# First expert of a routed network: its list of tokens taken behind round two of four, gathered before the search ends; eleven low parts made by GpSimd

## The chip, the cores and the metric

The kernel runs on one core of one Trainium2 chip. The metric is the device time of one execution in microseconds (us). A core has five engines that work beside each other, each through its own instructions in order: TensorE (PE, with its weight loads as PEld), VectorE (DVE), ScalarE (ACT), GpSimd (POOL) and SyncE (SP), which here issues loads. DMA queues move data between them and the chip's memory.

## What is computed

An attention over pooled keys and values gives 4608 tokens of 512 numbers. A gate scores each token against 8 experts. In the order of falling scores, a pair (token, expert) is taken if the token is free and the expert has fewer than 576 tokens. Each expert is a network of two layers, run on its own tokens alone.

```python
logits = x @ w_gate
order = np.argsort(-logits.flatten())
for idx in order:
    tok, e = (int(idx) // E, int(idx) % E)
    if assigned[tok] >= 0 or counts[e] >= cap:      # cap = 4608 // 8 = 576
        continue
    assigned[tok] = e
    counts[e] += 1
for e in range(E):
    mask = assigned == e
    out[mask] = np.maximum(x[mask] @ w1[e], 0.0) @ w2[e]
```

## The kernel before, in words

**Stages.** Attention runs over 36 tiles of 128 tokens and stores each tile of x in memory (`xd`). Then the experts run one after the other, each in two stages of products on TensorE, while the search for the next expert's tokens runs in between on VectorE and TensorE. No sort is made: the search finds which expert fills up first and at which score.

**The search** (`Routing.search`). The best score of each token is scaled to a number `q`. A round compares all q with 32 thresholds (`cmp`, VectorE), counts the tokens over each threshold for each expert (36 small products into `rt`, TensorE), asks which counts exceed what the expert still takes (`g`), and by one product and a maximum gets `up`, the step of the threshold. The next round divides that step by 32 again. There are four rounds. Behind the fourth, `sel` marks the tokens over the threshold and `full` the expert that is full.

**The close** (`Routing.close`). `fm` names the expert, `own` marks its tokens, `inc` and `si` number them by a running sum, `eid` is the expert's number as an address. The list itself is made by products with zero-one matrices: `OHb` holds which block of 32 entries a token falls in, and its number, `OHa` the place in the block. Nine products give the list, eight small ones (with `spread`) turn it into `rows`, the row numbers of five tiles of at most 128 tokens. For the first expert this is done in two parts, of two and three tiles. The rest of the close sums up what each expert still takes (`left`), checks (`bad`), and takes the chosen tokens and the full expert out of the scores (`lg`).

**An expert** (`Experts`). SyncE loads the weights w1 behind `eid` (`load_1`, the first expert's in two halves) and w2 (`load_2`). Each f32 number is split in a high part (`w1h`, `w2h`, ScalarE) and a low part (`w1l`, `w2l`, VectorE: raw minus high), in eight pieces of 512 columns; a product of two such numbers is three products. GpSimd gathers the token rows (`xg`, one indirect DMA for each tile), TensorE transposes them (`tp`), ScalarE and VectorE make `xh` and `xl`. Stage one multiplies by w1: for f = 0 to 7, a block of twelve products (w1h by xh, w1l by xh, w1h by xl, four each) into a tile `h`, for the columns 0 to 256 (tiles 0 and 1) and for the columns 256 to 576. ScalarE writes `hh` from it and VectorE `hl`. Tiles `h` rotate through five buffers, so that a block starts when the fifth one before it has been read. Stage two multiplies by w2 and scatters the rows out.

**What sets the order.** Every engine's order is written out by the program. The function `experts` walks through the products of a stage, adds up what they take by its own estimate (`now`, `dve`, `ready`), and between two products issues what is due: steps of the search (each `yield` of `Routing` hands over such a step with estimates), pieces of the weights (`Pieces`), transposes (`turn`), and the low parts of h (`later`). Before the first expert's products it works off the list and the first two tiles, with warming products (`warm`) in between. For the first expert the blocks ran in halves: f 0 to 3 of the columns 0 to 256, f 0 to 3 of the rest, then f 4 to 7 of both.

If the check in `bad` is not zero at the end, all experts are run again one by one with an exact search.

Of the kernel before, what the change touches and what calls it, by code (L numbers as in the profile page):

```python
# [423 lines left out]
class Routing:  # L424
# [7 lines left out]
    def __init__(self, tc, cst, wk, psR, lg, cap):  # L432
        self.tc, self.nc, self.cst, self.wk, self.psR = tc, tc.nc, cst, wk, psR
        self.lg = lg
        self.poke = None
        self.NC = lg.shape[1]
        self.cap = cap
# [175 lines left out]
    def search(self, shadow, spare):  # L613
# [18 lines left out]
        for k in range(rounds):  # L632
# [15 lines left out]
            else:  # L648
                compare(0, 2, 5, nb)
            if 0 < k < rounds - 1:  # L650
# [32 lines left out]

# [12 lines left out]
            nc.vector.tensor_reduce(up, ps[:, :8], axis=AX.X, op=OP.max)  # L696
            if k + 1 < rounds:
# [5 lines left out]
        nc.vector.tensor_scalar(self.sel, q16, up, 1.0 + EDGE, op0=OP.subtract, op1=OP.is_gt)  # L703

# [10 lines left out]
    def close(self, k, last):  # L715
# [7 lines left out]
        if k:  # L723
            nc.vector.tensor_tensor(self.code, self.code, new, op=OP.add)
        own = wk.tile([128, NC], F32, name="own")
        nc.vector.tensor_scalar(own, self.code if k else new, fm, None, op0=OP.is_equal)

        inc = wk.tile([128, NC], BF, name="inc")
        nc.vector.tensor_tensor_scan(inc, self.ones[:, :NC], own, 31.0, op0=OP.mult, op1=OP.add)
        eid = wk.tile([1, 1], I32, name="eid", bufs=3)  # L730
        nc.vector.tensor_scalar(eid, fm[:1], -1.0, 8.0, op0=OP.mult, op1=OP.add)
        nc.vector.tensor_scalar(eid, eid, 7.0, None, op0=OP.min)
        self.eid = eid
        yield 2.2, 2.2, "id"
        if not k:
            nc.vector.tensor_tensor(self.code, self.code, new, op=OP.add)
        ps = self.psum()
        nc.tensor.matmul(ps[:, :1], self.untri, self.ones[:, :1], start=True, stop=False)
        nc.tensor.matmul(ps[:, :1], self.tri, inc[:, NC - 1:NC], start=False, stop=True)

        si = wk.tile([128, NC], I32, name="si")
        nc.vector.scalar_tensor_tensor(si, inc, ps[:, :1], own, op0=OP.add, op1=OP.mult)
        sab = wk.tile([128, 2, NC], I32, name="sab")
        nc.vector.tensor_scalar(sab[:, 1], si, 5, None, op0=OP.arith_shift_right)
        nc.vector.tensor_scalar(sab[:, 0], si, 31, None, op0=OP.bitwise_and)
        sf = wk.tile([128, 2, NC], F16, name="sf")
        nc.vector.tensor_copy(sf.rearrange("p v (b q) -> p v b q", q=4), sab.rearrange("p v (q b) -> p v b q", q=4))
        if self.poke:

# [753 lines left out]
```

## Time and profile before

| what | value |
|---|---|
| runs before the change | 611.56 to 613.07 us, median 612.68 |
| profiled execution | 612.35 us, of which the span of the profile is 609.9 us |
| share of the span that is busy: PE, DVE, ACT, POOL | 97%, 65%, 39%, 29% |
| mean granted TensorE clock | 0.984 |
| stage-one products (L1093), three groups of 512 | 93.2, 93.4, 91.0 us |
| stage-two products (L1127), three groups of 256 | 101.8, 101.4, 101.5 us |
| low part of w1 (L1049, VectorE) | 64 of 685 ns |
| low part of w2 (L1058, VectorE) | 64 of 682 ns |
| low part of h (L1101, VectorE) | 128, mean 451 ns |
| gathers (L1037, GpSimd) | 40, mean 982 ns to issue |

The profile is of one execution. A row of its timeline gives the start and the length of an instruction in us from the span's start, the engine, the line of the kernel, the operation, out<-in by the program's names with their sizes, and in brackets how long the engine had been idle and what it had waited for. A row of stretches gives the busy time of each engine in a stretch of time. Groups of one line (page and groups) give count, busy time, mean length in ns and the idle time before them. TensorE is busy nearly always, so only the time in which it isn't can be saved: most of that lies between the end of attention (some 135 us) and the first expert's products.

### The profile page before, as it was taken

Reading aid. Unit: us, or ns where it says so; the run is one execution under the profiler, and the core shown is the slowest. Engines: PE = TensorE matmul, PEld = TensorE weight load, DVE = VectorE, ACT = ScalarE, POOL = GpSimd, SP = SyncE. Lnnn points to the kernel's source line nnn. Section 1 sums busy time; section 2 is a strip of 40 time slices with the busy share of each in tenths; the row PEclk is TensorE's granted clock in tenths of the full one; section 3 lists DMA queues with packets and bytes.
Section 4 is the critical chain, followed back from the end, with each engine's and each line's share of the span. In section 5 each row is a group of like instructions: output and inputs, shape, how many; then the busy total and the mean of one; then the engine's idle time right before and its main releaser. Section 6 shows DMA issues by size and latency. Waiting matters only on the chain.

```text
span 609.9 us, 11520 instructions
## 1 busy us (share of the span) xinstructions
PE 591.5 (97%) x4340; PEld 518.3 (85%) x4340; DVE 396.1 (65%) x1164; ACT 240.0 (39%) x562; POOL 177.3 (29%) x222
## 2 busy tenths in 40 slices
PE   8999999985999999999999999999999999999996
PEld 5999999983797799779977987898799889888975
DVE  7578888987885778767964976487367328503500
ACT  7444444461461434233432452255135325513411
POOL 2999999001200500420312301130221123011012
PEclk9999999995999999999999999999999999999999
DMA  8999972223531740616403701540081037014011
GB/s 353 419 420 423 397 274 82 77 100 98 167 116 31 254 147 22 213 62 219 134 35 116 284 1 52 207 174 18 36 323 57 34 120 278 2 52 166 1 40 43
DMA packets 32641, 92.23 MB, mean 151 GB/s; under 512 B 3488, under 2 KB 3488, under 8 KB 29888
## 3 DMA queue, kind: packets, MB, share of 16 engines
q1 hardware_dynamic: 21296, 62.92, 27.5%
q0 software_dynamic: 5952, 19.01, 9.2%
q10 hardware_dynamic: 5328, 9.48, 4.1%
q8 instruction: 35, 0.57, 0.4%
q14 instruction: 30, 0.25, 0.1%
HBM read 72.53 MB, written 18.87 MB: 150 GB/s over the span
## 4 chain that ended last, share of the span: by engine, by line
PE 81%; issue 7%; DVE 4%; DMA 3%; POOL 3%; ACT 1%; SPq 0%; POOLq 0%; ACTq 0%; another core or an unknown queue 0%; DVEq 0%
PE h L1093 32%; PE h L1127 25%; PE psa L272 6%; PE pss L227 5%; PE h L1132 4%; PE tp L1069 3%; DMA rawk<-in_k_dram 2%; PE pse L256 2%; PE rt L256 1%; PE rt L668 1%; DMA out_dram<-yt,rows 1%; PE rt L630 1%; DMA xg<-xd,rows 1%; PE rt L217 1%; DVE e L238 1%
## 5 line engine op out<-in xcount | busy, mean ns | idle before, releaser
L1127 PE MATMUL h<-w2l,hh 128*128 128x512 f32 x256 | 101.8, 398 | 0.0
L1127 PE MATMUL h<-w2h,hh 128*128 128x512 f32 x256 | 101.4, 396 | 0.3 <-PEq L1193 0.3
L1127 PE MATMUL h<-w2h,hl 128*128 128x512 f32 x256 | 101.5, 396 | 0.0
L1107 POOL DMA_INDIRECT out_dram<-yt,rows x29 | 30.3, 1045 | 232.3 <-ACT yt L1141 231.9
L1098 ACT ACTIVATE hh<-h 128x320 fp32r<-128x320 f32 (+1 forms) x128 | 52.5, 410 | 106.6 <-PE h L1093 103.3
L1093 PE MATMUL h<-xh,w1h 128*128 128x320 f32 (+1 forms) x512 | 93.2, 301 | 0.2 <-ACT xh L1071 0.2
L1093 PE MATMUL h<-xl,w1h 128*128 128x320 f32 (+1 forms) x512 | 93.4, 300 | 0.0
L1101 DVE SCALAR_TENSOR_TENSOR hl<-h,hh 128x320 fp32r<-128x320 f32 (+1 forms) x128 | 57.2, 451 | 53.1 <-ACT hh L1098 34.6
L1093 PE MATMUL h<-xh,w1l 128*128 128x320 f32 (+1 forms) x512 | 91.0, 298 | 0.0
L1093 PEld LDWEIGHTS h<-xh,w1h 128*128 128x128 f32 x512 | 75.7, 190 | 3.4 <-issue 2.7
L1093 PEld LDWEIGHTS h<-xl,w1h 128*128 128x128 f32 x512 | 76.1, 190 | 0.4
L1093 PEld LDWEIGHTS h<-xh,w1l 128*128 128x128 f32 x512 | 75.8, 189 | 0.0
L1037 POOL DMA_INDIRECT xg<-xd,rows x40 | 39.3, 982 | 101.9 <-DVE halves L806 52.7
L1141 ACT ACTIVATE yt<-h 128x512 f32<-128x512 f32 x32 | 19.1, 598 | 112.1 <-PE h L1127 67.4
L272 PE MATMUL psa<-vblk,eT 128*128 128x146 f32 (+3 forms) x390 | 59.9, 302 | 0.2
L1127 PEld LDWEIGHTS h<-w2h,hh 128*128 128x128 f32 x256 | 48.2, 188 | 9.3 <-issue 0.7
L1127 PEld LDWEIGHTS h<-w2l,hh 128*128 128x128 f32 x256 | 48.3, 189 | 8.8
L1127 PEld LDWEIGHTS h<-w2h,hl 128*128 128x128 f32 x256 | 48.2, 188 | 8.8
L272 PEld LDWEIGHTS psa<-vblk,eT 128*128 128x128 f32 (+1 forms) x390 | 50.9, 180 | 1.8 <-issue 0.3
L1049 DVE TENSOR_TENSOR w1l<-raw,w1h 128x512 fp32r<-128x512 f32 x64 | 41.7, 685 | 13.4 <-ACT w1h L1045 13.1
L1073 DVE TENSOR_TENSOR xl<-tp,xh 128x512 fp32r<-128x512 f32 (+1 forms) x40 | 25.3, 633 | 37.4 <-ACT xh L1071 37.3
L1058 DVE TENSOR_TENSOR w2l<-raw,w2h 128x512 fp32r<-128x512 f32 x64 | 43.2, 682 | 2.0 <-ACT w2h L1055 1.8
(224 smaller groups left out, 903.3 us busy)
## 6 DMA issues: line engine op xcount, KB each, us to landing
raw<-in_moe_w_dram SPq DMA_DIRECT2D x64, 512.0 KB, 6.3
xd<-xt ACTq DMA_DIRECT2D x36, 256.0 KB, 5.6
rawv<-in_v_dram SPq DMA_DIRECT2D x7, 1280.0 KB, 14.1
rawk<-in_k_dram SPq DMA_DIRECT2D x7, 1152.0 KB, 11.7
rawq<-in_q_dram SPq DMA_DIRECT2D x7, 1152.0 KB, 11.8
rawk<-in_k_dram SPq DMA_DIRECT2D x2, 576.0 KB, 4.7
rawv<-in_v_dram SPq DMA_DIRECT2D x1, 768.0 KB, 8.0
rawq<-in_q_dram SPq DMA_DIRECT2D x1, 640.0 KB, 9.0
```

The costliest lines, as they stand in the source:

```text
L227: nc.tensor.matmul(ps[cols, j // 2, 144 * (j % 2):144 * (j % 2) + 144], self.q_of(b, j, n, cols.stop - cols.start), self.kblk[b % 4][:, j] ...
L272: self.nc.tensor.matmul(o[h], self.eT[i][:, c, h], self.vblk[b % 4][:, self.BLOCKS[c]:self.BLOCKS[c + 1]], start=(c == cs[0]), stop=(c == ...
L1037: nc.gpsimd.indirect_dma_start(out=self.xg[:n, t, :], out_offset=None, in_=self.xd, in_offset=bass.IndirectOffsetOnAxis(ap=rows[:n, t:t + ...
L1049: self.nc.vector.tensor_tensor(l, raw, h.bitcast(F32), op=OP.subtract)
L1058: self.nc.vector.tensor_tensor(self.w2l[:, i], self.raw2[e][:, i], self.w2h[:, i].bitcast(F32), op=OP.subtract)
L1073: later(1.3, 0.65, lambda: nc.vector.tensor_tensor(xl, ps[:, :, :n], xh, op=OP.subtract))
L1093: nc.tensor.matmul(ps[:, :m], a[:, j, fs], b[:, j, o], start=(n == 0), stop=(n == 11))
L1098: nc.scalar.activation(hh[:, f, o], ps[:, :m], AF.Relu)
L1101: later(0.65, 0.4, lambda f=f, o=o, m=m, ps=ps: nc.vector.scalar_tensor_tensor(hl[:, f, o], ps[:, :m], 0.0, hh[:, f, o].bitcast(F32), op0= ...
L1107: st = nc.gpsimd.indirect_dma_start(out=rows, out_offset=bass.IndirectOffsetOnAxis(ap=idx, axis=0), in_=y, in_offset=None)
L1127: nc.tensor.matmul(ps, a[:, f, o], b[:, f], start=(f == 0 and k == 0), stop=(f == 7 and k == 2))
L1132: nc.tensor.matmul(ps[64 * a:64 * a + 64, :256], self.hr[:, f], self.raw2[e][:, f, 256 * a:256 * a + 256], start=(f == 0), stop=(f == 7))
```

## The change

The first expert's search is cut open behind its second round.

- **The early list** (`early`). What lies over the threshold of round two is taken as the first expert's already. From these tokens `eid`, `si` and two parts of the list are made, for the tiles 0 and 1 and the tiles 2 and 3 (512 tokens), and gathered. The rounds three and four come behind that in program order; the second part's small products stand within round three.
- **The late list** (`close` with `late`). Behind round four the tokens that are not among the first 512 (`taken`) get a short list of 64 for the fifth tile. Seven steps (`odd`) check that nothing else differs.
- **Stage one of the first expert** runs the blocks of the columns 0 to 256 four at a time, by kind: for f 0 to 3 all w1h by xh, then all w1l by xh, then all w1h by xl; then f 4 to 7; then the columns 256 to 576 for all f one by one.
- **GpSimd** makes three low parts of w1 and all eight of w2 for the first expert, eleven in all. VectorE made them before.
- Other experts keep their order but for one place where waiting low parts of x are issued by a fixed product (`lowered`).

```diff
@@ search @@
             else:
                 compare(0, 2, 5, nb)
+                if k == 2:
+                    rest = self.list_part(8, 16, self.bank)
+                    next(rest)
...
                 count(early, NC)
+                if k == 2:
+                    yield from rest
...
             nc.vector.tensor_reduce(up, ps[:, :8], axis=AX.X, op=OP.max)
+            if k == 1 and not spare:
+                yield from self.early(ps, up, q16)
...
+    def early(self, ps, up, q16):
+        nc, wk, NC = self.nc, self.wk, self.NC
+        full = wk.tile([128, 8], F32, name="full")
+        nc.vector.scalar_tensor_tensor(full, ps[:, :8], up, self.wts, op0=OP.is_ge, op1=OP.mult)
+        sel = wk.tile([128, NC], BF, name="sel")
+        nc.vector.tensor_scalar(sel, q16, up, 1.0 + EDGE, op0=OP.subtract, op1=OP.is_gt)
+        self.fm0 = fm = wk.tile([128, 1], F32, name="fm")
+        nc.vector.tensor_reduce(fm, full, axis=AX.X, op=OP.max)
+        own = wk.tile([128, NC], F32, name="own")
+        nc.vector.scalar_tensor_tensor(own, self.want, fm, sel, op0=OP.is_equal, op1=OP.mult)
+        inc = self.scan(own)
+        self.name(fm)
+        yield 2.2, 2.2, "id"
+        si = self.order(inc, own)
+        self.planes(si)
+        self.rows = wk.tile([128, 5], I32, name="rows", bufs=3)
+        self.block(0, 8)
+        self.number(0, 8)
+        self.lanes()
+        self.block(8, 16)
+        yield 2.6, 2.6
+        part = self.list_part(0, 8, self.bank)
+        next(part)
+        self.number(8, 16)
+        yield 0.6, 0.6
+        yield from part
+        self.taken = wk.tile([128, NC], F32, name="taken", bufs=1)
+        nc.vector.scalar_tensor_tensor(self.taken, si, 32.0 + 512.0, own, op0=OP.is_lt, op1=OP.mult)
...
@@ close, late @@
+        if late:
+            more = wk.tile([128, NC], F32, name="moreown", bufs=1)
+            nc.vector.scalar_tensor_tensor(more, self.taken, 0.0, own, op0=OP.is_equal, op1=OP.mult)
+            both, own = own, more
...
+        if late:
+            odd = wk.tile([128, 3], F32, name="odd", bufs=1)
+            nc.vector.tensor_tensor(both, both, self.taken, op=OP.subtract)
+            nc.vector.tensor_reduce(odd[:, 0:1], both, axis=AX.X, op=OP.min)
+            nc.vector.tensor_reduce(odd[:, 1:2], si, axis=AX.X, op=OP.max)
+            nc.vector.tensor_tensor(odd[:, 2:3], fm, self.fm0, op=OP.subtract)
+            nc.vector.scalar_tensor_tensor(self.bad, odd[:, 0:1], odd[:, 0:1], self.bad, op0=OP.mult, op1=OP.add)
+            nc.vector.scalar_tensor_tensor(self.bad, odd[:, 1:2], 32.0 + 64.0, self.bad, op0=OP.is_ge, op1=OP.add)
+            nc.vector.scalar_tensor_tensor(self.bad, odd[:, 2:3], odd[:, 2:3], self.bad, op0=OP.mult, op1=OP.add)
...
@@ Experts.low1, low2 @@
-        self.nc.vector.tensor_tensor(l, raw, h.bitcast(F32), op=OP.subtract)
+        (eng or self.nc.vector).tensor_tensor(l, raw, h.bitcast(F32), op=OP.subtract)
...
@@ stage1 @@
-        for o, some in ((cols[0], range(4)), (cols[1], range(4)), (cols[0], range(4, 8)), (cols[1], range(4, 8))) if (
-                halves) else ((cols[0], range(8)), (cols[1], range(8))):
+        for o, u in ((slice(0, 256), together), (slice(256, 576), 1)):
...
+            for f0 in range(0, 8, u):
+                ps = {}
+                for k, (a, b) in enumerate(((self.w1h, self.xh), (self.w1l, self.xh), (self.w1h, self.xl))):
+                    for f in range(f0, f0 + u):
...
@@ experts @@
-    for i in range(4):
-        w1.next(i < 3)
-    since[0, "rows"] = -7.0
-
+    turned[0] = 0
+    since[0, "rows"] = -7.0
+    for i in range(4):
+        w1.up()
     step(0)
-    warm(6)
+    step(0)
+    warm(4)
+    X.load_1(behind(0), 2, 4)
+    w1.next(False)
+    w1.next(False)
     now = dve = -1.0
-    for t in range(2):
-        turn(0, t)
-        warm(2)
-    flush()
+    turn(0, 0)
+    w1.next(False)
     step(0)
+    turn(0, 1)
+    flush(1)
+    w1.next(False)
+    warm(2)
...
-        w2 = Pieces(e, X.high2, X.low2)
-        for n, dt in enumerate(X.stage1(later, not e)):
+        w2 = Pieces(e, X.high2, X.low2, not e)
+        for n, dt in enumerate(X.stage1(later, 1 if e else 4)):
...
+            if not e and n == 22:
+                for i in range(4, 7):
+                    X.high1(0, i)
+                    X.low1(0, i, nc.gpsimd)
+                w1.h = w1.l = 7
+            if not e and n == 46:
+                w1.next()
```

The helpers `scan`, `name`, `order`, `planes`, `block`, `number`, `lanes` and `list_part` hold the same steps as the close did before, cut up for use in both places.

**TensorE before the first product.** The names: `g` and `ones` make the sums behind a round, `ones` into `h` is a warming product, `tp` are a tile's transposes, `cmp` a count. Before:

```order
L798 MATMUL rt<-cp,spread 128x3
...
L526 MATMUL h<-ones 128x512
...
L1069 MATMUL tp<-ident,xg 128x128 x4
...
L526 MATMUL h<-ones 128x512
...
L1069 MATMUL tp<-ident,xg 128x128 x4
...
L814 MATMUL rt<-pc,ones 128x8
L1093 MATMUL h<-xh,w1h 128x256 x4
L1093 MATMUL h<-xh,w1l 128x256 x4
```

And now, from the end of round three:

```order
L812 MATMUL h<-cp,spread 128x2
L699 LDWEIGHTS ones
L699 MATMUL rt<-g_247,ones 128x8
...
L527 MATMUL h<-ones 128x512
L1145 MATMUL tp<-ident,xg 128x128 x4
L631 LDWEIGHTS cmp
L631 MATMUL rt<-oh_259,cmp 32x8
...
L1145 MATMUL tp<-ident,xg 128x128 x4
...
L1170 MATMUL h<-xh,w1h 128x256 x2
L699 LDWEIGHTS ones
L699 MATMUL rt<-g_248,ones 128x16
L1170 MATMUL h<-xh,w1h 128x256 x14
```

The 36 counting products of round four stand between the transposes of the first and the second tile; the sum behind that round stands within the first block. The warming products are four and two, where they were six, two and two.

**VectorE in the close, around the low part of the block f = 4.** `left` to `lg` is the close, `odd` the new check, `hl` the low part of h. Before, at the end of the close:

```order
L825 TENSOR_REDUCE two<-sel 128x1
L826 SCALAR_TENSOR_TENSOR bad<-two,bad 128x1
L829 TENSOR_SCALAR pick<-full,fm 128x8
...
L838 TENSOR_TENSOR lg<-lg,pen_2143 128x288
L839 TENSOR_TENSOR lg<-lg,pen_2145 128x288
L1101 SCALAR_TENSOR_TENSOR hl<-h,hh 128x256
```

And now:

```order
L893 SCALAR_TENSOR_TENSOR bad<-two,bad 128x1
L896 TENSOR_TENSOR own<-own,taken 128x36
L897 TENSOR_REDUCE odd<-own 128x1
L898 TENSOR_REDUCE odd<-si 128x1
L899 TENSOR_TENSOR odd<-fm 128x1
L900 SCALAR_TENSOR_TENSOR bad<-odd,bad 128x1
...
L914 TENSOR_TENSOR lg<-lg,pen_2357 128x288
L915 TENSOR_TENSOR lg<-lg,pen_2359 128x288
L1182 SCALAR_TENSOR_TENSOR hl<-h,hh 128x256 x3
```

The low parts of the blocks f = 4 to 6 now stand behind the close with its seven more steps. On TensorE the block that takes the buffer of f = 4 is h_2405 (names with their numbers, from the close's sum on; h_2252 is f = 4, h_2382 and h_2405 are f = 0 and 1 of the columns 256 to 576):

```order
L880 MATMUL rt_2333<-pc_2308,ones_74 128x8
L1170 MATMUL h_2252<-xl_2062,w1h_2021 128x256
L1170 MATMUL h_2264<-xl_2062,w1h_2021 128x256 x4
L1170 MATMUL h_2269<-xl_2062,w1h_2021 128x256 x4
L1170 MATMUL h_2296<-xl_2062,w1h_2021 128x256 x4
L1170 MATMUL h_2382<-xh_2061,w1h_2021 128x320 x4
L1170 MATMUL h_2382<-xh_2061,w1l_2022 128x320 x4
L1170 MATMUL h_2382<-xl_2062,w1h_2021 128x320 x4
L1170 MATMUL h_2405<-xh_2061,w1h_2021 128x320 x4
```

Between the sum and h_2405 stand 13 products of 256 and 12 of 320 columns.

**GpSimd.** `norow` is a small gather whose data nobody uses. Before, the five gathers stood together and the first scatters followed; now:

```order
L1233 DMA norow<-in_moe_w_dram,sab 32x512
L1113 DMA xg<-xd,rows 128x512 x4
L1125 TENSOR_TENSOR w1l<-raw_1892,w1h 128x512 x3
L1113 DMA xg<-xd,rows 64x512
L1134 TENSOR_TENSOR w2l<-raw_2288,w2h 128x512 x8
L1187 MEMSET spacer 1x1
```

The fifth gather stands behind three low parts of w1, the eight of w2 behind that gather.

More of the change, by code (lines that the diff above doesn't have):

```diff
@@ L713, in chosen, with close @@
         return pc
-    def close(self, k, last):
+    def close(self, k, last, late=False):
         nc, wk, NC, lg = self.nc, self.wk, self.NC, self.lg
@@ L722, in close @@
         nc.vector.tensor_tensor(new, sel, self.want, op=OP.mult)
-        if k:
+        if not late:
             nc.vector.tensor_tensor(self.code, self.code, new, op=OP.add)
         own = wk.tile([128, NC], F32, name="own")
[L726 to L730, printed above, removed]
@@ L812, in close @@
+        self.number(0, n)
+        self.lanes()
+        yield (2.1, 2.1) if late else (2.6, 2.6)
+        part = self.list_part(0, n, self.psum, 5 - n // 4)
+        next(part)
+        if not late:
+            self.pc = self.chosen(sel)
+        yield (0.6, 0.6) if late else (1.75, 1.75)
+        yield from part
+        if late:
+            nc.vector.tensor_tensor(self.code, self.code, new, op=OP.add)
+            self.pc = self.chosen(sel)
             yield 1.15, 1.15
-            ps = self.psum()
@@ L885, in phase @@
             pass
-        yield from self.close(k, last)
+        yield from self.close(k, last, k == 0)
     def suspect(self):
@@ L1254, in step @@
                 toks[p] = R.rows, R.halves
-                turned[p] = 0
+                turned.setdefault(p, 0)
+                if not p:
+                    what = "late"
         since[p, what] = now
@@ L1322, in turn @@
         nonlocal now
-        now = max(now, since[e, "rows"] + 6.0 + 1.3 * t) + 0.45
+        now = max(now, comes(e, t)) + 0.45
         flush(1)
@@ L1328, in turn, with comes @@
         if (e, t) == (0, 2):
-            later(1.0, 0.2, lambda: X.load_1(behind(0), 2, 4))
-        elif (e, t) == (0, 4):
             later(1.0, 0.2, lambda: X.load_2(behind(1)))
+    def comes(e, t):
+        if (e, t) == (0, 4):
+            return since[0, "late"] + 3.7 if 0 in toks else 1e9
+        return since[e, "rows"] + 6.0 + 1.3 * t
     def turns(e, upto, late):
@@ L1336, in turns @@
         t = turned.get(e, 5)
-        if t < upto and due(e, "rows", 6.5 + 1.3 * t) and now >= last + 1.4 and (fresh or through or t < late):
+        if t < upto and (e or (0, "late") in since) and (e, "rows") in since and now >= comes(e, t) + 0.5 and now >= last + 1.4 and (fresh or through or t < late):
             last = now
@@ L1343, in warm @@
         R.warm(n, psB.tile([128, 512], F32, name="h", bufs=5))
[L1345 removed]
+    R.bank = lambda: psB.tile([128, 512], F32, name="h", bufs=5)
+    while R.found[1] < 4:
         step(0)
```

240 lines of the change are left out of this document (135 added, 105 removed).

## The prediction

> **What bounds the kernel.** I read the page's chain first, then busy time by stretches, then the timeline of the 30 us in which attention ends and the first expert begins.
>
> ```profile
> PE 81%; issue 7%; DVE 4%; DMA 3%; POOL 3%; ACT 1%; SPq 0%; POOLq 0%; ACTq 0%; another core or an unknown queue 0%; DVEq 0%
> ...
> 140.00:145.00 5.00, 2.64 (x62) 2.28 (x61) 3.39 (x19) 0.00 (x0) 0.00 (x0) 0.50 0.01 3
> ...
> 157.12:185.40 28.28, 28.28 (x226) 27.59 (x227) 24.37 (x75) 14.63 (x37) 0.00 (x0) 1.00 0.34 119
> 185.40:605.50 420.10, 419.59 (x2893) 361.66 (x2891) 247.16 (x746) 151.46 (x357) 78.19 (x113) 1.00 0.33 113
> ```
>
> TensorE carries 81% of the chain that ended last. The stretches give start:end, length, busy time of PE, PEld, DVE, ACT and POOL, granted clock, DMA. TensorE is busy through all 28.28 us of the first expert's stage one and 419.59 of the 420.10 us behind it. Only the hole before 157.12 can be won; and what stage two of the first expert starts earlier is won at the end, unless something behind it is late.
>
> The hole is a chain: four rounds (`up` ends each), the list (`rows`), the gather, the transposes, the first product.
>
> ```profile
> 138.60 0.14 DVE L696 TENSOR_REDUCE up<-rt 128x1 f32<-128x8 f32 x1
> ...
> 143.91 0.17 DVE L696 TENSOR_REDUCE up<-rt 128x1 f32<-128x8 f32 x1 [0.26 <-PE rt L694]
> 144.52 0.20 DVE L722 TENSOR_TENSOR new<-sel,want 128x36 f32<-128x36 bf16 x1
> 145.33 0.14 DVE L732 TENSOR_SCALAR eid<-eid 1x1 int32<-1x1 int32 x1
> 146.85 1.00 SPq L1020 DMA_DIRECT2D raw<-in_moe_w_dram  x2
> 149.33 0.16 DVE L802 TENSOR_SCALAR rows<-rt 128x2 int32<-128x2 f32 x1
> ...
> 150.34 0.97 POOL L1037 DMA_INDIRECT xg<-xd,rows  x1 [3.10 <-DVE rowd L782]
> 151.05 2.72 PE L526 MATMUL h<-ones 128*128 128x512 bf16 x6
> 151.18 2.38 ACT L1045 ACTIVATE w1h<-raw 128x512 fp32r<-128x512 f32 x4 [12.34 <-DMA raw<-in_moe_w_dram]
> 151.62 0.95 POOL L1037 DMA_INDIRECT xg<-xd,rows  x1 [0.30 <-issue]
> 153.83 0.68 PE L1069 MATMUL tp<-ident,xg 128*128 128x128 f32 x4
> 155.78 0.66 PE L1069 MATMUL tp<-ident,xg 128*128 128x128 f32 x4 [0.83 <-DMA xg<-xd,rows]
> 157.12 0.74 PE L1093 MATMUL h<-xh,w1h 128*128 128x256 f32 x4 [0.25 <-ACT xh L1071]
> ```
>
> Round two's `up` starts at 138.60, round four's at 143.91: the two rounds that the list no longer waits for are 5.31 us.
>
> **The start.** From `up` to `rows` it took 5.42. The early list needs the same steps without `new` (0.20): rows at 138.60 + 5.22 = 143.82. The gather began 1.01 behind rows and the next 1.28 behind it, now 144.83 and 146.11; their data were there 3.49 and 4.16 behind their starts, now 148.32 and 150.27. The weights came 1.52 + 4.33 behind `eid`, the expert's number, which moves up by as much: by 146.
>
> TensorE is not there that soon, for its order puts rounds three and four in between. One round, and the small products that turn list entries into rows:
>
> ```profile
> 136.41 0.90 DVE L625 TENSOR_TENSOR cmp<-q,j 128x256 bf16<-128x256 f16 x3
> 136.76 1.36 PE L630 MATMUL rt<-oh,cmp 128*32 128x8 bf16 x36 [0.88 <-DVE cmp L625]
> ...
> 138.15 0.15 DVE L687 TENSOR_TENSOR g<-rt,need 32x8 bf16<-32x8 f32 x1 [0.35 <-PE rt L630]
> ...
> 148.70 0.59 PE L798 MATMUL rt<-cp,spread 128*128 128x2 f16 x8 [0.51 <-DVE cp L786]
> ```
>
> VectorE makes `taken` and q (some 0.6), then compares from 144.45; TensorE counts from 144.8 (0.35 behind) to 146.15, turns the list's second half (0.59) to 146.75; rows and g bring it to 147.05, the product behind g to 147.25. Four warming products (0.43 each) last to 149.0. The first transposes (0.68, a little more at half clock) end near 149.8, round four's count (1.36) at 151.2, and only then come the second tile's transposes; its data have been there since 150.3. From there to the first product it was 157.12 - 155.78 = 1.34. **First product at 152.54 instead of 157.12: 4.58 us won**, not 5.31.
>
> **More products in stage one.** Its pace before, free of other work and with a block of nine search products between:
>
> ```profile
> 162.99 0.64 PE L1093 MATMUL h<-xh,w1h 128*128 128x256 f32 x4
> ...
> 164.42 0.75 PE L1093 MATMUL h<-xh,w1h 128*128 128x320 f32 x4
> ...
> 166.18 0.75 PE L1093 MATMUL h<-xh,w1h 128*128 128x320 f32 x4
> ...
> 177.79 0.46 PE L1093 MATMUL h<-xh,w1h 128*128 128x320 f32 x2
> ...
> 179.88 0.75 PE L1093 MATMUL h<-xh,w1h 128*128 128x320 f32 x4
> ```
>
> Twelve products of 256 columns take 1.43 (0.12 each), of 320 columns 1.76 (0.147), and 2.09 with the block: such a block costs 0.33. New are one of nine and one of eight for the late list, and three single steps (round four's, the late list's order, the close's sum) that I put at 0.1 each: about **+0.95** (0.7 to 1.2).
>
> **The fifth tile.** Its rows wait in VectorE's order behind the eighth low part of w1, that behind ScalarE's eighth high part, that behind the third block's output.
>
> ```profile
> 158.86 0.38 ACT L1098 ACTIVATE hh<-h 128x256 fp32r<-128x256 f32 x1 [1.79 <-PE h L1093]
> ...
> 161.14 0.13 DVE L1351 COPY late<-eid 1x1 int32<-1x1 int32 x1
> 162.25 0.97 SPq L1020 DMA_DIRECT2D raw<-in_moe_w_dram  x2
> 166.09 1.16 ACT L1045 ACTIVATE w1h<-raw 128x512 fp32r<-128x512 f32 x2 [1.09 <-DMA raw<-in_moe_w_dram]
> 167.42 1.29 DVE L1049 TENSOR_TENSOR w1l<-raw,w1h 128x512 fp32r<-128x512 f32 x2
> ...
> DMA to landing us min/median/max: 2.7/3.4/7.3
> ...
> L173 POOL TENSOR_TENSOR tk<-tk 128x576 f32<-128x576 f32 x7 | 9.9, 1410 | 0.5
> ...
> L187 POOL TENSOR_TENSOR vsum<-t 128x320 f32<-128x320 f32 x7 | 6.0, 862 | 0.5
> ```
>
> The third block ends near 158.5 (152.54, then 44 products of 0.12 and the insertions); 0.38 + 0.58 + 0.65 later the rows follow, with the gaps between at 160.3, and 0.3 on (the pause between gathers) the gather. Landing takes 2.7 to 3.4: 163.3 to 164.0, and half a tile is nearest the short end. TensorE asks behind 73 products, the insertions and two transposes (0.45 beside other products, 0.66 at most), at 163.1 to 163.5: **+0.25** (0 to 0.9).
>
> This covers two edits that I cost at nothing. The weights' second half: `late` is copied near 149.2, and 1.11 + 3.84 later, at 154.2, the data are there, before ScalarE's and TensorE's first need of them (near 159.5). GpSimd's three low parts of w1, which stand ahead of the late gather in its queue: by the two rows 512 columns cost some 1.27, so they end near 159, ahead of the rows. Without that cover each microsecond there is one of TensorE's. The eight low parts of w2 (10 us) follow ScalarE's high parts one by one, and the last is asked for 5 us into stage two.
>
> **A tile buffer.** Five buffers carry `h`. The block h_2405 (columns 256 on) takes the one of h_2252 (f = 4), which is free when VectorE has made that block's low part. VectorE's order now has the close, with seven steps more, ahead of it.
>
> ```profile
> 156.70 0.17 PE L814 MATMUL rt<-pc,ones 128*128 128x8 bf16 x1
> ...
> 157.71 0.15 DVE L816 TENSOR_TENSOR left<-need,rt 128x8 f32<-128x8 f32 x1
> ...
> 159.34 0.46 DVE L838 TENSOR_TENSOR lg<-lg,pen 128x288 f32<-128x288 f32 x1
> ...
> 160.21 0.42 DVE L1101 SCALAR_TENSOR_TENSOR hl<-h,hh 128x256 fp32r<-128x256 f32 x1
> ```
>
> Eleven steps took 159.34 - 157.71 = 1.63, so seven more are 1.05, or 1.2 since three of them form a chain. Left can start 0.2 behind the sum's product (0.17); to the low part 2.50 + 1.2, the part 0.42: free 4.35 behind the sum. TensorE comes after 13 x 0.12 + 12 x 0.147 = 3.35. **+1.0** (0.6 to 1.3). Expert two's first compare then ends, laid out the same way, some 4.95 behind that low part and is asked for 32 x 0.147 = 4.7 behind it: **+0.2** (0 to 0.5). From the third round on its search stands in stage two where it stood.
>
> **The clock.**
>
> ```profile
> 136.50:137.00 0.50, 0.24 (x7) 0.24 (x8) 0.50 (x3) 0.50 (x4) 0.00 (x0) 0.86 0.72 274
> ...
> 153.50:154.00 0.50, 0.44 (x2) 0.17 (x2) 0.50 (x2) 0.06 (x1) 0.46 (x1) 0.57 0.74 131
> ```
>
> It was halved near 136.9 and whole again near 153.9, 2.9 behind the first warming product. Now four warming products from 147.25 are followed by counting products, beside which the clock stayed halved in rounds three and four. If it comes up before 151, nothing is lost; if only some 2.9 behind the steady products of 152.5, half of that and 0.4 of the transposes. I take **+0.45** (0 to 1.9), nearer to the first, since two thirds of that time are warming and transposes.
>
> [...]
>
> **The sum.** -4.58 + 0.95 + 0.25 + 1.0 + 0.2 + 0.45 = -1.73. The profiled execution took 612.35 (0.33 under the median of the runs, 612.68): **610.6**. With all low ends it is -3.3, with all high ends +1.2: 609.1 to 613.6. A measurement can tell some 0.3% from no change, 1.84 us: under 610.84 is faster, over 614.52 slower.
>
> **Rivals.**
> *Nothing waits*: the clock is up in time, the buffer free and the late tile there. Only the added products remain: 612.35 - 4.58 + 0.95 = 608.7, with what lies beside it 608.4 to 609.6. For it: TensorE's stage one had no idle time before. Against: the buffer would have to come free a quarter of its 4.35 sooner. 0.17.
> *Forecast*, 609.6 to 611.3: 0.48.
> *Most of it is lost*: a clock that rises behind 155 and a late tile at 3.4 or more: -4.58 + 0.95 + 0.9 + 1.2 + 0.4 + 1.4 = +0.3, so 611.3 to 613.6, about 612.6. For it: the halved clock beside counts. 0.27.
> *Slower*: VectorE's steps stretch beside GpSimd's low parts. Those fill 11 x 1.27 = 14 us, in which VectorE, busy 24.37 of 28.28 before and now without eleven parts of 0.65, works some 10; its search of expert two and its low parts hold TensorE where the waits above already are. Stretched by half, +5 us: 615.6; it decides from a third on (3.6 us to reach 614.5). Against: no row shows a stretch. 0.06.
> [...]
> *It doesn't do what it says*: if fewer than 512 tokens are known, the check sends all experts through the exact path, some 450 us more, near 1060. On the reference's inputs 574 of 576 are known behind round two. 0.02.
>
> Faster: 0.17 + 0.34 of the forecast = 0.51; within 0.3%: 0.14 + 0.27 + 0.01 = 0.42; slower 0.07. For 8 in 10 the range is 608.6 to 613.0.
>
> **What would show it.** The second round's `up` some 5 us ahead of the first gather; the second tile's transposes waiting for the count and not for data; first product near 152.5 to 153; a wait of 0 to 1 at the fifth tile; about 1 us of idle TensorE at the second block of 320 columns, behind VectorE's low part of f = 4; stage two near 183.5 instead of 185.40. The prediction is wrong if TensorE never waits there, if VectorE's compares or GpSimd's parts last over 1.3 times the rows above, or if expert two's stage one begins with a wait.

## The result, and the profile after

The changed kernel is slower: 621.49 us median of 6 runs (618.31 to 623.08) against 612.66 (611.56 to 613.07), a ratio of 1.014 with a 95% interval of 1.0109 to 1.017. The forecast was 610.6, the range 608.6 to 613.0. The profiled execution took 623.08, its span is 621.3; it is the slowest of the six, with a mean granted clock of 0.975.

Again the page's chain, then stretches (start:end, length, busy time of PE, PEld, DVE, ACT, POOL, granted clock, DMA) with the borders that the new trace gives:

```profile
PE 81%; DVE 7%; issue 6%; DMA 4%; ACT 1%; POOL 1%; POOLq 0%; ACTq 0%; another core or an unknown queue 0%; DVEq 0%
...
154.12:196.15 42.03, 34.66 (x249) 32.75 (x248) 31.76 (x92) 15.21 (x38) 14.76 (x13) 0.85 0.22 75
196.15:616.25 420.10, 419.55 (x2891) 361.61 (x2891) 247.43 (x748) 150.76 (x356) 78.88 (x113) 1.00 0.33 113
```

VectorE's share of the chain has gone from 4% to 7%. Everything behind stage one is as it was: 419.55 us of TensorE in 420.10. So the loss lies ahead of it, and the first expert's stage one carries all of it: it took 28.28 us with TensorE always busy, and takes 42.03 with TensorE idle for 42.03 - 34.66 = 7.37, at a mean clock of 0.85. Put together against before: first product 3.00 earlier (154.12 for 157.12), idle +7.37, busy 34.66 - 28.28 = +6.38, in all +10.75. The two profiled executions differ by 10.73.

The idle time is three waits, all for VectorE. TensorE's timeline (start, length, engine, line, operation, and in brackets the idle time ahead and who ended it):

```profile
162.88 0.39 PE L798 MATMUL rt<-OHb,OHa 128*128 128x16 f16 x9 [2.61 <-DVE OHa L786]
...
175.99 0.85 PE L1170 MATMUL h<-xh,w1h 128*128 128x320 f32 x4 [0.70 <-DVE hl L1182]
...
185.01 0.42 PE L672 MATMUL rt<-oh,cmp 128*128 128x32 bf16 x9 [4.06 <-DVE cmp L626]
```

The second is the tile buffer of the prediction (forecast +1.0). The first stands ahead of the late list, the third ahead of expert two's first count. What VectorE did before them, and GpSimd beside it:

```profile
158.31 3.75 POOL L1125 TENSOR_TENSOR w1l<-raw,w1h 128x512 fp32r<-128x512 f32 x3 [7.56 <-ACT w1h L1121]
...
158.32 1.38 DVE L770 CAST sf<-sab 128x72 f16<-128x72 int32 x1
159.73 1.21 DVE L858 TENSOR_TENSOR OHb<-sf,blk 128x144 f16<-128x144 f16 x1
160.97 1.19 DVE L781 TENSOR_TENSOR OHb<-OHb,tokv 128x144 f16<-128x144 f16 x1
162.08 0.75 DVE L786 TENSOR_TENSOR OHa<-sf,j 128x1152 f16<-128x1152 f16 x1
...
176.48 7.49 POOL L1134 TENSOR_TENSOR w2l<-raw,w2h 128x512 fp32r<-128x512 f32 x6 [9.01 <-ACT w2h L1131]
...
177.92 0.80 DVE L1182 SCALAR_TENSOR_TENSOR hl<-h,hh 128x256 fp32r<-128x256 f32 x2
...
179.04 0.44 DVE L574 TENSOR_REDUCE bv<-lg 128x36 f32<-128x288 f32 x1
179.52 0.82 DVE L586 TENSOR_SCALAR q<-bv,lo,scale 128x36 f32<-128x36 f32 x1
180.37 1.20 DVE L592 TENSOR_SCALAR q32c<-q 128x36 f32<-128x36 f32 x1
181.61 1.19 DVE L579 CAST q16a<-q32c 128x36 f16<-128x36 f32 x1
182.71 1.58 DVE L580 TENSOR_TENSOR oh<-lg,bv 128x288 bf16<-128x288 f32 x1
184.21 0.74 DVE L626 TENSOR_TENSOR cmp<-q16a,j 128x1152 bf16<-128x1152 f16 x1
```

Three GpSimd parts of 1.25 us run from 158.31 to 162.06; three VectorE steps beside them end at 159.70, 160.94 and 162.16, each some 0.1 behind the end of a part, however small the step is. Once the parts are through, OHa, the largest, takes its usual 0.75. The same at 176.48: the cast and one of the scalings of 128x36 elements last 1.2 us, the other 0.82 (0.18 and 0.30 in the first experiment below), while a reduction (bv, 0.44) and a step that takes one input from PSUM, the memory of TensorE's products (hl, 0.40 each), are not touched.

The 6.38 us more of busy time are not all work. The granted clock by half microseconds shows it halved three times:

```profile
135.50:136.00 0.50, 0.26 (x5) 0.19 (x4) 0.47 (x4) 0.49 (x3) 0.00 (x0) 0.81 0.00 0
156.00:156.50 0.50, 0.50 (x5) 0.50 (x4) 0.43 (x4) 0.00 (x0) 0.00 (x0) 0.71 0.77 299
163.00:163.50 0.50, 0.50 (x11) 0.50 (x10) 0.17 (x1) 0.00 (x0) 0.00 (x0) 0.62 0.00 0
166.50:167.00 0.50, 0.50 (x6) 0.50 (x5) 0.50 (x2) 0.19 (x1) 0.45 (x1) 0.97 0.00 0
183.50:184.00 0.50, 0.00 (x0) 0.00 (x0) 0.50 (x1) 0.00 (x0) 0.47 (x1) 0.60 0.00 0
190.00:190.50 0.50, 0.50 (x4) 0.31 (x3) 0.03 (x1) 0.34 (x2) 0.00 (x0) 0.58 0.00 0
```

All other slices from 130 to 205 show 1.00 or 0.50, so one of 0.81 was whole for 0.31 of its half microsecond: the clock fell at 135.81 and rose at 156.29, fell at 163.12 and rose at 166.53, fell at 183.60 and rose at 190.42. The second fall comes 0.24 behind the end of the first wait (162.88), the third within the third wait (180.95 to 185.01).

### The profile page after: what moved, and what is told of

It reads as the page before. It is cut to its first block, busy times and chain, and to the rows that moved or that the text cites. A ratio compares the mean times of both kernels' runs of the same rounds, so it can differ in the third digit from the quotient of the medians.

```text
span 621.3 us, 11578 instructions
## 1 busy us (share of the span) xinstructions
PE 596.8 (96%) x4355; PEld 523.4 (84%) x4355; DVE 401.8 (65%) x1178; ACT 239.7 (39%) x562; POOL 191.9 (31%) x233
## 4 chain that ended last, share of the span: by engine, by line
PE 81%; DVE 7%; issue 6%; DMA 4%; ACT 1%; POOL 1%; POOLq 0%; ACTq 0%; another core or an unknown queue 0%; DVEq 0%
PE h L1170 30%; PE h L1208 25%; PE psa L272 6%; PE pss L227 5%; PE h L1213 4%; PE tp L1145 3%; DMA rawq<-in_q_dram 3%; PE pse L256 2%; PE rt L256 1%; PE rt L672 1%; DMA out_dram<-yt,rows 1%; PE rt L631 1%; PE rt L217 1%; DMA rawk<-in_k_dram 1%; DVE e L238 1%
## 5 line engine op out<-in xcount | busy, mean ns | idle before, releaser
L1170 PE MATMUL h<-xh,w1h 128*128 128x320 f32 (+1 forms) x512 | 94.5, 305 | 0.7 <-DVE hl L1182 0.7
L1170 PE MATMUL h<-xl,w1h 128*128 128x320 f32 (+1 forms) x512 | 94.7, 305 | 0.0
L1170 PEld LDWEIGHTS h<-xh,w1h 128*128 128x128 f32 x512 | 77.2, 194 | 4.5 <-issue 2.7
L1125 DVE TENSOR_TENSOR w1l<-raw,w1h 128x512 fp32r<-128x512 f32 x61 | 40.1, 685 | 14.8 <-ACT w1h L1121 14.7
L227 PE MATMUL pss<-kblk,rawq 128*128 128x144 f32 (+1 forms) x320 | 44.0, 294 | 0.9 <-DMA rawq<-in_q_dram 0.7
```

The costliest lines, as they stand in the source:

```text
L227: nc.tensor.matmul(ps[cols, j // 2, 144 * (j % 2):144 * (j % 2) + 144], self.q_of(b, j, n, cols.stop - cols.start), self.kblk[b % 4][:, j] ...
L1125: (eng or self.nc.vector).tensor_tensor(l, raw, h.bitcast(F32), op=OP.subtract)
L1170: nc.tensor.matmul(p[:, :m], a[:, j, fs], b[:, j, o], start=(k == j == 0), stop=(k == 2 and j == 3))
```

## The experiments

The theory (A): while GpSimd makes a low part, a VectorE step of certain kinds doesn't get through until that part has ended; the two long waits and the two later falls of the clock follow from it. Rivals: (B) the clock alone, with its late rise; (C) the new order of blocks and the longer close. All ratios are against the kernel before on the same chip, with 95% intervals.

**All eleven low parts back on VectorE**, at the same places of the program:

```diff
-                    X.low1(0, i, nc.gpsimd)
+                    X.low1(0, i, nc.vector)
...
-                self.low(self.e, self.l, nc.gpsimd)
+                self.low(self.e, self.l, nc.vector)
```

> All eleven low parts back on VectorE, at the same places of the program; nothing else moves on any engine's order. Theory A (a VectorE step of certain kinds cannot start until the GpSimd part that is running ends; so GpSimd's parts hold VectorE's list steps and expert two's first compare): the two stalls of TensorE (2.61 us before the late list's small products, 4.06 us before expert two's first count) go, and so does what the clock lost behind them; 610.5 to 613.5, that is 612.35 less 3.0 for a first product at 154.1, plus the worked-out additions of some 2.5. Theory B (the clock gate alone: a late and halved start of stage one): the stalls are only where the loss shows, 618 to 622. Theory C (the order of blocks and the seven more steps of the close): 617 to 621, with the wait at the tile buffer as large as before.

612.97 us, ratio 1.0014 (1.0002 to 1.0025). Of the 1.4% lost 0.14% are left, by nothing but the engine of eleven instructions; rivals B and C fall, since the order of blocks, the close and a late clock (whole at 154.33, 1.5 behind the first product; in the change 2.2) are still there. VectorE's steps have their lengths again and TensorE's waits are small:

```profile
156.74 0.23 DVE L770 CAST sf<-sab 128x72 f16<-128x72 int32 x1
...
175.48 0.18 DVE L579 CAST q16a<-q32c 128x36 f16<-128x36 f32 x1
...
171.02 0.85 PE L1170 MATMUL h<-xh,w1h 128*128 128x320 f32 x4 [0.68 <-DVE hl L1182]
...
177.35 0.39 PE L672 MATMUL rt<-oh,cmp 128*128 128x32 bf16 x9 [1.38 <-DVE cmp L626]
```

The first product comes at 152.81, 1.3 ahead of what my expectation took from the change's profile, yet stage two begins at 186.33 (185.40 before): even so nothing is won. The time fell into the expected range by two misses that partly cancel, for stage one takes 5.2 us more than before and not some 2.5. What is left waits for VectorE, which in this stage is busy for 29.55 us against 24.37 before:

```profile
152.81:186.33 33.52, 30.89 (x248) 29.03 (x248) 29.55 (x102) 15.15 (x38) 1.00 (x2) 0.98 0.26 92
```

**Only the eight of w2, and only the three of w1, back on VectorE** (one of the two lines each).

> Only the eight low parts of w2 back on VectorE; the three of w1 stay on GpSimd. Theory A: the stall before expert two's first count (4.06 us) goes with the halved clock behind it (about 2.3), the stall of 2.61 before the late list's products stays: 614 to 616.5. Theories B and C: 618 to 622.

> Only the three low parts of w1 back on VectorE; the eight of w2 stay on GpSimd. Theory A: the cast of sf, OHb and its product by tokv take 0.2 to 0.5 us again instead of 1.2 to 1.4, the first stall goes, the second stays: 616.5 to 619.5. The sum of the gains of this run and of the run with w2 alone put back should be that of both put back, within 1 us, if the two stalls stand for themselves. Theories B and C: 619 to 622.

617.48, ratio 1.0083 (1.0061 to 1.0105), and 618.34, 1.0099 (1.0081 to 1.0117). The first is a microsecond over what I expected, the second within it. Each keeps just its own long wait: with w1 on GpSimd 2.52 us before the late list's products, with w2 there 4.00 us before expert two's first count. By the ratios (1.014 for the change) the gains are 0.57% and 0.41%, together 0.98% where both gave 1.26%: 1.7 us apart, more than the 1 I had allowed. Part of it shows in the first one's profile: behind its 2.52 the clock stayed halved for 6.83 us (161.09 to 167.92), where the change's profile has 3.41. The change's own two sets of runs lie 0.4% apart (below), so this doesn't decide whether the two waits stand quite for themselves.

**The low parts in quarters.** GpSimd keeps all eleven but makes each in four instructions:

```diff
-        (eng or self.nc.vector).tensor_tensor(l, raw, h.bitcast(F32), op=OP.subtract)
+        for s in (slice(128 * c, 128 * c + 128) for c in range(4)) if eng else (slice(None),):
+            (eng or self.nc.vector).tensor_tensor(l[..., s], raw[..., s], h[..., s].bitcast(F32), op=OP.subtract)
```

> GpSimd keeps all eleven low parts, but makes each in four instructions of 128 columns. If a VectorE step waits until the running GpSimd instruction ends (theory A), the waits fall from up to 1.25 us to some 0.35 us a step: the cast of sf near 0.5, the first stall under 1, the second near 1.5, 613 to 617. If the two engines share a port in proportion, or GpSimd holds it from its first instruction to its last, nothing changes: 620 to 623.

613.43, ratio 1.0034 (1.0018 to 1.005), in the range of theory A; the two waits are 0.42 and 0.70. It is the length of one GpSimd instruction that VectorE waits for, not GpSimd's work, of which there is more now (the twelve quarters of w1 took 5.62 us instead of 3.75):

```profile
157.36 0.37 DVE L770 CAST sf<-sab 128x72 f16<-128x72 int32 x1
157.77 0.39 DVE L858 TENSOR_TENSOR OHb<-sf,blk 128x144 f16<-128x144 f16 x1
...
175.29 0.38 DVE L579 CAST q16a<-q32c 128x36 f16<-128x36 f32 x1
175.59 0.78 DVE L580 TENSOR_TENSOR oh<-lg,bv 128x288 bf16<-128x288 f32 x1
```

Each of these steps lasts 0.15 to 0.35 longer than alone, not 1.0.

**The check steps later.** As the quarters, with the seven steps `odd` put into a function that expert two's second round calls, between its count and `g`:

```diff
+            def check():
+                nc.vector.tensor_tensor(both, both, self.taken, op=OP.subtract)
...
+            self.check = check
...
                 next(shadow, None)
+                if k == 1 and self.check:
+                    self.check()
+                    self.check = None
                 yield 0.45, 0.9
```

> The run in quarters, with the seven check steps (odd) moved from the end of the close into expert two's second round. If those steps make the buffer of f = 4 late (the prediction's term of +1.0), TensorE's 0.68 us at the second block of 320 columns goes to 0 to 0.1, and its 0.70 before expert two's first count shrinks, since VectorE reaches the first compare up to 1.2 us sooner: 612.0 to 612.8 where the quarters gave 613.4. If the wait hangs on something else, 613.2 to 613.7 with the same gap.

614.78, ratio 1.0046 (1.0029 to 1.0064): my expectation missed, though its mechanism was there. TensorE no longer waits at the second block of 320 columns, so the check did make that buffer late. But two other waits came: 1.49 us for `g`, behind the moved steps, and 3.67 us for the fifth tile. For half of that one GpSimd's queue is the reason:

```profile
156.49 5.52 POOL L1132 TENSOR_TENSOR w1l<-raw,w1h 128x128 fp32r<-128x128 f32 x12 [7.22 <-ACT w1h L1127]
162.16 0.93 POOL L1119 DMA_INDIRECT xg<-xd,rows  x1 [0.16 <-issue]
...
159.93 0.14 DVE L820 TENSOR_SCALAR rows<-rt 128x1 int32<-128x1 f32 x1
...
166.27 0.55 PE L1153 MATMUL tp<-ident,xg 64*128 64x64 f32 x4 [3.67 <-DMA xg<-xd,rows]
```

The rows were there at 159.93, the gather stood behind the quarters of w1 until 162.16, 2.23 later; where the queue is free it begins 0.4 behind the rows. That is 1.8 of the 3.67. The data came 4.11 behind the gather's start, where four other profiles show 2.95 to 2.99; why stays open. The rest is TensorE, which came early in this execution, with the clock whole at 149.4; where it starts later the wait is smaller (0.48 in the run before).

**w1 on VectorE, w2 in quarters**, check steps as in the last run.

```diff
-                    X.low1(0, i, nc.gpsimd)
+                    X.low1(0, i)
```

> As the run before it (quarters, check steps later), but w1's three low parts stay on VectorE. Theory A: in the late list nothing waits for GpSimd, the gap of 0.42 us before its nine products falls away, but VectorE has 2.0 us more in that place: 611.3 to 612.5. If w1's parts cost VectorE more than GpSimd's quarters hold it up: 612.5 to 613.5.

613.14, ratio 1.0016 (1.0003 to 1.0029), a time that I had given to the other reading; the waits speak for theory A. Those at the late list and the fifth tile are 0.24 each, none at the buffer and none before the first count; what is left is one wait of 1.50 us for `g`, behind the seven steps.

**GpSimd's parts in the kernel before.** Nothing of the change but w2's eight parts:

```diff
-        self.nc.vector.tensor_tensor(self.w2l[:, i], self.raw2[e][:, i], self.w2h[:, i].bitcast(F32), op=OP.subtract)
+        (self.nc.vector if e else self.nc.gpsimd).tensor_tensor(self.w2l[:, i], self.raw2[e][:, i], self.w2h[:, i].bitcast(F32), op=OP.subtract)
```

> The kernel before, with one thing changed: the first expert's eight low parts of w2 are made by GpSimd. Theory A: they hold VectorE there too, in expert two's rounds, whose compares TensorE's counts wait for: 613.5 to 617, with steps of 0.2 us of VectorE that last 1.0 to 1.6. If GpSimd's parts are harmful only together with the early list (no slack left on VectorE): 611 to 612.5, for VectorE has 5.5 us less to do.

612.22, ratio 1.0013 (1.0003 to 1.0022): the first reading is wrong, the second holds. VectorE is held just as long there:

```profile
166.17 0.75 DVE L625 TENSOR_TENSOR cmp<-q16a,j 128x1152 bf16<-128x1152 f16 x1
...
170.80 9.34 POOL L1058 TENSOR_TENSOR w2l<-raw,w2h 128x512 fp32r<-128x512 f32 x7 [15.04 <-ACT w2h L1055]
...
174.63 1.27 DVE L699 TENSOR_SCALAR q<-q32c,up 128x36 f16<-128x36 f32 x1
175.94 1.80 DVE L625 TENSOR_TENSOR cmp<-q,j 128x1152 bf16<-128x1152 f16 x1
```

but TensorE has no idle row in that stretch. The first round's compare (166.17) is through before GpSimd begins; the held steps are those of the second round, whose count TensorE's order asks for late enough. In the changed kernel the same parts begin at 176.48, ahead of the first round's steps. The price of a held step is set by who waits for it.

**Copies instead of subtractions.** All low parts on VectorE, and GpSimd copies each high part of w2 (448 columns, one input) to a tile that nobody reads.

```diff
+                side = wk.tile([128, 448], F32, name="side", bufs=1)
+                nc.gpsimd.tensor_copy(side, X.w2h[:, self.l, :448].bitcast(F32))
```

> The run with all eleven low parts on VectorE, and beside it GpSimd copies each of the eight high parts of w2 (448 columns) to a tile that nobody reads: one input instead of two, at the time of the low parts. If any arithmetic of GpSimd holds VectorE, its steps near expert two's first compare last to the end of a copy and the time is 615 to 620; if it takes GpSimd's second input, 612.5 to 613.5 as without the copies.

615.26, ratio 1.0047 (1.003 to 1.0064), at the low end of the first reading. Few of VectorE's steps stand beside a copy (0.56 long when nothing disturbs it):

```profile
172.59 0.56 POOL L1380 COPY side<-w2h 128x448 f32<-128x448 f32 x1 [8.41 <-ACT w2h L1131]
...
172.87 0.30 DVE L610 TENSOR_SCALAR steps<-shares,width 128x4 f32<-128x4 f32 x1
...
173.60 0.70 DVE L1134 TENSOR_TENSOR w2l<-raw,w2h 128x512 fp32r<-128x512 f32 x1
...
173.83 0.90 POOL L1380 COPY side<-w2h 128x448 f32<-128x448 f32 x1
...
176.65 0.18 DVE L579 CAST q16a<-q32c 128x36 f16<-128x36 f32 x1
...
177.12 0.68 DVE L1134 TENSOR_TENSOR w2l<-raw,w2h 128x512 fp32r<-128x512 f32 x1
177.12 1.10 POOL L1380 COPY side<-w2h 128x448 f32<-128x448 f32 x1 [0.77 <-ACT w2h L1131]
177.72 1.11 DVE L626 TENSOR_TENSOR cmp<-q16a,j 128x1152 bf16<-128x1152 f16 x1
...
178.88 0.39 PE L672 MATMUL rt<-oh,cmp 128*128 128x32 bf16 x9 [1.82 <-DVE cmp L626]
```

The cast keeps its length, but it fell into the pause between two copies (176.35 to 177.12), so it tells nothing. Two steps that began during a copy are longer: `steps` (0.30 for 0.23) ends just behind the copy, and the compare (1.11 for 0.75) ends 0.61 behind one. (A scaling, `q`, began during a copy and kept its 0.30; it ended 0.05 behind that copy.) The subtractions with two inputs, which now are VectorE's, keep their 0.7, and here the copies wait: five copies began while a subtraction ran, and each ended 0.42 behind that subtraction's end (174.73 behind 174.31, 178.22 behind 177.80). So in these rows the hold goes both ways: the copy or the step that began second waited. The kernel before with w2's parts on GpSimd fits that: seven parts in a row took 9.34 there, with the compare of 175.94 beside them, 0.60 more than seven at the change's pace (six in 7.49). A copy, with its one input, holds VectorE too, as far as these two steps show.

TensorE waits 1.82 instead of 1.38, so that is 0.4 of the 2.0 us more (0.33% by the ratios). Behind the wait the clock fell, at 180.23, and rose at 183.65, which it had not done behind 1.38. It had also first risen at 156.34, 2.01 later than in the profile of the run without copies; the first copy starts at 172.59, so the copies have no part in that.

**The check as a step of its own.** As the run with w1 on VectorE, with the seven steps ahead of expert two's fourth round and counted by the planner:

```diff
+            if spare and k == 3 and self.check:
+                self.check()
+                self.check = None
+                yield 0.0, 1.2
```

> w1's low parts on VectorE, w2's in quarters on GpSimd, and the seven check steps as a step of their own ahead of expert two's fourth round, counted in the planner's estimates. The gap of 1.50 us before the second round's g of the run before goes, nothing takes its place: 611.3 to 612.3. If the seven steps cost TensorE the same wherever they stand (VectorE is the bound of this stage): 612.8 to 613.5.

611.87, ratio 1.0001 (0.9991 to 1.0011), as expected: the 1.50 us are gone, and no wait in stage one is over 0.42. The profiled execution took 609.64 and is the shortest of its set. Its stage one:

```profile
151.59:182.67 31.08, 30.08 (x248) 28.31 (x248) 26.67 (x88) 14.63 (x38) 13.75 (x28) 1.00 0.30 105
```

Two of the ten executions of this kernel took 2021 and 3280 us. They are left out of the ratio (the median of the other eight is 611.70). No profile covers them, and the cause is open: the exact path, which the prediction puts near 1060, doesn't give these times, and the next kernel, which holds the same edits, had none in 12. A kernel that may do this isn't ready for use, whatever its median.

**Four warming products more**, in the 2.3 us before the early list's products, and the fifth tile's transposes asked for 1.5 us later:

```diff
         yield 2.6, 2.6
+        self.warm(4, self.bank())
         part = self.list_part(0, 8, self.bank)
...
-            return since[0, "late"] + 3.7 if 0 in toks else 1e9
+            return since[0, "late"] + 5.2 if 0 in toks else 1e9
```

> As the run before it, with four warming products more, in the 2.3 us in which TensorE waits for the early list's OHa, and the fifth tile's transposes asked for 1.5 us later. If the clock comes up for lack of work of that size (the prediction's clock term: halved until 1.5 to 2.8 us behind the first product), it is whole before the first product, transposes take 0.66 instead of 1.11, the first product comes at 151.8 to 152.2, and the first sixteen products take 1.9 instead of 2.3 to 3.2: 609.3 to 611.0. If four products in a hole do not lift it: within 0.4 of the run before.

610.74 (608.91 to 612.73), ratio 0.9987 (0.9973 to 1.0000): the best of all, some 0.1% under the kernel before, at the edge of what the interval allows. Its mechanism I can't claim: in its profile the clock rose at 154.21, no sooner than without the warming products, and the first product came at 152.39, later than expected. That the time lies in the range is luck as far as the clock goes.

**The changed kernel again**, for a second profile.

> The changed kernel once more, for a second profile beside these: the 1.4 us that the second list part's rows waited behind their products, with GpSimd issuing a gather, were absent in the four profiles with the same start. If they are a matter of some executions, rows follow their products at once here, the first product comes near 152.8 and the time is 618 to 622; if they belong to this kernel, the same gap and 620 to 623.

618.74 (616.07 to 622.18), ratio 1.0103 (1.0073 to 1.0133). The waits are the same (2.52, 0.69, 4.08). The second list part's rows follow their products at once here (146.97, after products that began at 146.47), the first product comes at 153.05. In the first profile they waited:

```profile
146.21 0.46 PE L812 MATMUL h<-cp,spread 128*128 128x2 f16 x8
...
146.62 0.95 POOL L1113 DMA_INDIRECT xg<-xd,rows  x1 [0.30 <-issue]
...
148.08 0.16 DVE L817 TENSOR_SCALAR rows<-h 128x2 int32<-128x2 f32 x1 [1.42 <-PE h L812]
```

None of the ten other profiles with this code has these 1.42 us, so they are of that execution; what held the step there stays open. The change's ten executions fall near 616 to 619 (four) or near 621 to 623 (six), and the clock parts them: its mean is 0.983 to 0.986 in the four and 0.975 to 0.978 in the six. A mean of 0.975 over 621.3 us means 2 x 0.025 x 621.3 = 31 us at half clock (the profile's three stretches make 30.7), one of 0.983 over 617.1 means 21. Which stretch was shorter or missing in the four, no profile shows. Both profiles are of the longer kind, so what they show of the clock's part is the larger of the two.

## Why the prediction was wrong

**What failed** is the sentence that the low parts given to GpSimd cost nothing because they end ahead of what asks for them. I looked at who waits for the parts, not at what VectorE does beside them. The mechanism stood among the rivals, as "VectorE's steps stretch", but with the wrong law: a stretch by half, 5 us, deciding from a third on. The runs show, in place of a cost of nothing, waits of TensorE for VectorE of 2.61 us and, beyond the 1.38 that stay with the parts on VectorE, 2.68. VectorE's steps there last to the end of the running part, 1.19 for 0.18 us. So what counts is how many short steps in a chain fall beside long parts: three before the late list, five before expert two's first compare. That rival gave 615.6 and a chance of 0.06; as a wait for the end of a part of 1.27 (my price from two rows of GpSimd's arithmetic; 1.25 measured) it would have given three and five times about a microsecond, and the sign.

My row against it, that no row shows a stretch, was no evidence. In the profile of before GpSimd computes beside VectorE in attention (the two rows of it in the prediction are from there), but the VectorE steps beside it take an input from PSUM or reduce: `e`, which reads PSUM, and the reduction `mx` took 0.76 us each beside GpSimd (31 to 45) and 0.76 with GpSimd idle (124.63 and 125.49). These two kinds are the ones that stay at their length here too (hl 0.40, bv 0.44, with GpSimd's parts and without).

The signs that I named looked elsewhere: the compare kept its 0.74, GpSimd's parts took 1.25 to 1.30 where I had 1.27, and TensorE waited at the buffer as forecast. Only the first product and the start of stage two (196.15, not 183.5) spoke against it.

What the runs show of the hold: beside parts of 1.25 us the casts `sf` and `q16a` took 1.38 for 0.23 and 1.19 for 0.18, the product of OHb by tokv 1.19 for 0.23, while the reduction bv kept its 0.44; beside quarters such a step took some 0.2 more instead of 1.0; and copies that began within a subtraction ended 0.42 behind it. Why these steps are held and the others not, no trace here shows.

Term by term:

| term | forecast | measured |
|---|---|---|
| first product | -4.58 (152.54) | 154.12 in the first profile of the change, 153.05 in the second; 152.38 to 152.87 in the first four experiments, 151.59 and 151.84 where the clock rose at 149.3 |
| more products in stage one | +0.95 | +1.80 (busy 30.08 against 28.28 at whole clock, the check as a step of its own) |
| fifth tile | +0.25 | no wait in the change, where TensorE itself came at 170.01 and not at 163.3; 0.16 to 0.48 where the late list is not held, 3.67 in one early start |
| tile buffer | +1.0 | 0.70; gone when the seven check steps are moved |
| expert two's first compare | +0.2 | 4.06; 1.38 with the parts on VectorE, 0 with quarters, w1 on VectorE and the check moved |
| low parts on GpSimd | 0 | 2.61 at the late list, and 4.06 - 1.38 = 2.68 at the first compare |
| clock | +0.45 | 1.09 at the start ((156.29 - 154.12) / 2), and two more falls |

The buffer and its reason were right. The start was right in size, partly by luck: in the first experiment the product behind g came at 146.51, 0.74 ahead of the forecast, and the transposes took 1.11 at half clock where I had a little over 0.68, so that the first product came 0.27 late. The missing wait at the fifth tile is luck too, since TensorE was held up itself. The added products were mis-sized by half: I priced them by a block of nine (0.33, so 0.04 each) and three single steps of 0.1, and 21 of them (the 248 of that row hold one product of stage two) took 1.80, 0.09 each; why they cost more than that block wasn't tried. The clock's term looked at the first rise alone; that a wait in stage one would halve it again was nowhere in the sum. Busy time above 30.08 and the 1.09 of the start is 34.66 - 30.08 - 1.09 = 3.5 us in this profile, a third of the loss. With the waits of 2.61 and 2.68 that makes some 8.8 us for the step that failed, an estimate; giving the eleven parts back to VectorE won 8.5 us between the medians and 7.7 by the ratios.

With most waits taken away the kernel is level with the one before: the ratio is 1.0001 with the check as a step of its own (1.00 us idle is left in its stage one) and 0.9987 with warming, where the forecast's -1.73 us would be 0.9972, outside both intervals, if only just outside the second. So the earlier start is real (4.3 us with all parts on VectorE), and what the change itself adds in stage one takes nearly all of it back.

## What to carry to other kernels

Before work moves to GpSimd, list the VectorE steps that will run beside it, and look for chains of short steps of the kinds that were held here: casts and scalings of 4 to 72 columns (`steps`, 4 columns, 1.05 for 0.23 us; sf, 72, 1.38 for 0.23), and steps with two inputs outside PSUM (OHb 1.21 for 0.23, oh 1.58 for 0.45). (Reductions, a reciprocal, a scaling of one column and steps with an input from PSUM kept their lengths: bv 0.44, scale 0.16, width 0.21, hl 0.40.) Here a step of a held kind lasted up to 1.15 us longer beside GpSimd instructions of 1.25, and up to 0.35 longer beside quarters, so cut GpSimd's work into short instructions or keep it away from such chains. A held step costs only if someone's order asks for its result then: w2's eight parts cost 0.9% here (618.34 against 612.97 with all on VectorE) and 0.1% in the kernel before. Price a wait of TensorE together with what the clock does behind it (3.4 or 6.8 us at half clock with the waits of 1.82 and more here).

## What the runs showed of the hardware

**The clock was halved for 3.41 us or a whole multiple of it.** In the change it was halved for 20.48 (135.81 to 156.29), 3.41 and 6.82 us, that is 6, 1 and 2 times 3.41. In other profiles the first of these stretches was 13.66 (check as a step of its own) and 17.06 (warming early; 17.07 in the kernel before), 4 and 5 times. With the same start of the first expert the clock was whole from 149.3 in one profile (check as a step of its own) and from 156.3 in another (the change). What sets the length of a stretch, no run here shows.

```profile
135.50:136.00 0.50, 0.00 (x0) 0.00 (x0) 0.43 (x3) 0.33 (x2) 0.00 (x0) 0.67 0.00 0
149.00:149.50 0.50, 0.50 (x17) 0.50 (x17) 0.50 (x2) 0.43 (x1) 0.26 (x1) 0.67 0.57 131
```

(check as a step of its own: fall at 135.67, rise at 149.33.)

**A short wait could cost more than itself.** Waits of 1.38 and 1.50 us in stage one left the clock whole; with waits of 1.82, 2.5 to 2.6, 3.67 and 4.0 to 4.1 it fell each time, within the wait or up to 1.35 us behind it, and stayed halved for 3.4 or 6.8 us. Between 1.50 and 1.82 nothing was measured, and whether it is the length of the wait alone that decides wasn't tried.
